# Sparse attention and a squared-ReLU layer on one core: longer DMA rows for v and k, larger mask, square and division operations, and a fifth block in the seven-product form

## The chip, the cores and the metric

The kernel runs on one core of a Trainium2 chip. The core has a matrix engine (PE, with its weight loads shown apart as PEld), a vector engine (DVE), a scalar engine (ACT), a general engine (POOL) and a queue engine (SP) that here only issues DMAs. Each takes its own instructions in order and waits for the others through semaphores. The metric is the device time of one launch in microseconds (us).

## The reference

Two stages follow each other. The first is attention over q, k and v of shape (8 batches, 8 heads, 576 positions, 64 features). Heads 0 to 3 see a band of the last 32 positions ("loc" in the code); heads 4 to 7 see every 32nd position back from the query ("str").

```
scores = q @ k^T / 8 ;  scores = where(mask, scores, -1e9)
attn   = exp(scores - max) ; attn = attn / (sum(attn) + 1e-9)
x      = (attn @ v), heads side by side : (4608 tokens, 512)
```

The second is a layer over all 4608 tokens: `h = x @ w_in` (512 to 2048), `g = s * relu(h)^2 + b`, `out = g @ w_out` (2048 to 512, fp32).

## The kernel before

All arithmetic on PE is in fp16 with fp32 sums. The tokens of the layer are cut into nine blocks T of 512 tokens. The first product of a block (F1, `ff1`, matmul at line 877) takes 16 feature tiles by four 128-row pieces of x, 64 matmuls of 512 columns. After each feature tile a ReLU out of PSUM is written to `u` (`rl`, line 899, ACT) and the square of `u` to `gT` (`sq`, line 908 on DVE, line 906 on ACT, which may take it from block `SEVEN` on). `u` has four buffers. The second product (F2, `ff2`, line 926) is again 64 matmuls of 512 columns, with an eviction on DVE (line 937) and a store for each of four token tiles. Blocks 5 to 8 (`SEVEN = 5`) do the second product in Strassen's manner (`ff2_seven`, line 845): seven products of half size, each 2 x 8 matmuls of 256 columns, out of sums of quarters of `gT` (`sums_post`, line 717, eight DVE operations a block) and differences of quarters of `w_out` (`mix_post`, line 739, four DVE operations, once, after the last plain block). Evictions of such a block are lines 764, 776 and 787.

The attention of a batch b is four pairs of heads m (0 and 1 loc, 2 and 3 str). A pair brings q and k into the layout "feature by position" (PE transposes at lines 403 and 411, or DMA transposes on SP), makes scores on PE (line 531, three groups of a PSUM bank each), takes their exponential on ACT (`ex`, line 547) and, from batch 1 on, multiplies with a 0/1 mask on DVE (`ms`, line 555), each group by itself, into one of six buffers per kind (`p_bufs`). The product with v (`av`, line 585) has a column of ones beside v, so that it also yields the sum; a reciprocal (line 600) and a multiplication (line 611) on DVE follow for each PSUM bank, one bank for a head of a loc pair, two for a head of a str pair. From batch 4 on these banks are `ps_a` and `ps_t` in turn. The result goes as x, transposed, into one of `NX = 4` slots of `xT`; the slot of batch b is free when F1 has read what lay there (`x_free`).

Loads are DMAs on POOL's queue that convert fp32 to fp16. Band k of batches 0 to 3 and all strided v of batches 0 to 3 come in long rows (several positions in one row) into a staging tile; k is then put side by side by copies (`pair_post`), v is copied into `v_str` (`cast_v`, line 315). From batch 4 on (`KB_DMA`, `LONG_V`) band k (line 270) and strided v (`load_vs`, line 298) come in rows of one position straight into their last layout, four DMAs for each tensor and batch; band k goes from there by a DMA transpose into `kT_loc`.

The order of all instructions is written by a planner (`Plan`) when the program is built. It keeps a time for each engine with assumed costs, emits PE steps one after another (attention when it is due by the progress of the layer, else F1, else F2) and gives DVE and ACT work to the engine that would end it first, in the order in which it becomes ready. On the chip every engine then keeps that order. A step of PE that comes before its inputs holds all PE work behind it.

Of the kernel before, what the change touches and what calls it, by code (L numbers as in the profile page):

```python
# [15 lines left out]
class Plan:  # L16
# [24 lines left out]
    def flush(self):  # L41
        while True:
# [13 lines left out]
            for k in p[3]:  # L56
                if isinstance(k, Group):
                    k = ("rel", k.tag, k.n)
                soon = isinstance(k, tuple) and k[0] == "soon"
                self.done[k] = end + (6000.0 if soon else p[4] or  # L60
                                           (5500.0 if eng == "D" and end < 110000.0 else self.LAT[eng]))

    def step_ready(self, s):
        r = self.ready_at(s.needs)
        if r is None:
            return None
        if s.group is not None:
            n = self.count.get(s.group.tag, 0)
            if n >= s.group.bufs:
                k = ("rel", s.group.tag, n - s.group.bufs)  # L70
                if k not in self.done:
                    return None
                r = max(r, self.done[k])
        return r

    def emit(self, s):
        if s.group is not None:
            s.group.n = self.count.get(s.group.tag, 0)
            self.count[s.group.tag] = s.group.n + 1
# [26 lines left out]
class Step:  # L106
    def __init__(self, fn, ns, needs=(), group=None, keys=(), posts=(), after=None):
        self.fn, self.ns, self.needs, self.group = fn, ns, needs, group
        self.keys, self.posts, self.after = keys, posts, after


@with_exitstack
def kernel(
# [46 lines left out]
    up = ctx.enter_context(tc.tile_pool(name="up", bufs=4))  # L160
# [24 lines left out]
    v_str = [const.tile([SQ, 4, ST, D + 1], FP16, name=f"v_str{i}") for i in range(NV)]  # L185
# [4 lines left out]
    NX = 4  # L190
# [5 lines left out]
    def x_free(b):  # L196
# [3 lines left out]
    p_bufs = {True: [const.tile([128, 3 * LQ + WIDE], FP16, name=f"p_loc{i}") for i in range(6)],  # L200
              False: [const.tile([SQ, 5 * SQ + WIDE], FP16, name=f"p_str{i}") for i in range(6)]}
# [3 lines left out]
    ks = [const.tile([SR, 4 * ST * D], FP16, name=f"ks{i}") for i in range(2)]  # L205
# [44 lines left out]
    for i in range(NV):  # L250
        nc.vector.memset(v_loc[i][:, :, :, D:D + 1], 1.0)
        nc.vector.memset(v_loc[i][0:LPAD, :, 0, :], 0.0)
        nc.vector.memset(v_str[i][:, :, :, D:D + 1], 1.0)
    for tl in p_bufs[True]:
        nc.vector.memset(tl[:, 4 * LQ:], 0.0)
    for tl in p_bufs[False]:
        nc.vector.memset(tl[:, 4 * SQ:], 0.0)
# [4 lines left out]
    def load_qk(b):  # L262
        for name, src in (("q", q), ("k", k)):
            tl = inp.tile([LQ, NL], FP16, tag=name + "l", name=name + "l")
            loaded[b, name + "l"] = tl
            if b >= (QB_DMA if name == "q" else KB_DMA):
# [28 lines left out]
    def load_vs(b):  # L295
        vs = v_str[b % NV]
        for h in range(4):
            nc.gpsimd.dma_start(  # L298
                out=vs[:, h, :, 0:D],
                in_=v[b, 4 + h].rearrange("(p j) d -> p j d", j=ST))  # L300

# [15 lines left out]
    def pair_post(b, name, mm, key):  # L317
# [4 lines left out]
        def g(eng):  # L322
            if paired[b, name] is None:
                paired[b, name] = inp.tile([128, 2, LT, 2 * D], FP16, tag="pp", bufs=3,
# [4 lines left out]
        plan.post([key], {"A": 810, "V": 350, **({"P": 900.0} if b in (1, 2, 3) else {})}, g,  # L329
                  [("in", name + "l", b, mm)])  # L330

    def cast_v(b, loc, mm, key):
        nt, np_, dst = (LT, 128, v_loc) if loc else (ST, SQ, v_str)

        def g(eng):
            src = vl_stage if loc else loaded[b, "vs"].rearrange(
                "p (h t d) -> p h t d", h=4, d=D)
            for h in range(2 * mm, 2 * mm + 2):
                copy_on(eng, out=dst[b % NV][0:np_, h, :, 0:D], in_=src[:, h])
        n = nt * D  # L340
        plan.post([key], {"P": 1000.0} if loc else {"A": 2 * (170 + 0.83 * n), "V": 540.0}, g,
# [4 lines left out]
    def rows_before(b, mm, key):  # L346
# [5 lines left out]
        def g(eng):  # L352
# [3 lines left out]

    TB, SB, AB, F1B, F2B = 1, 2, 1, 2, 2
# [3 lines left out]
          for tag, n in (("t", TB), ("s", SB), ("a", AB), ("f1", F1B), ("f2", F2B))}  # L361

    taken = {"a": 0, "t": 0, "s": 0}

    def group_of(kind, b, m, q=False):
# [3 lines left out]
        if b == 0:  # L369
            banks = {"a": [f2, f2, f1], "t": [t, a], "s": [("s", SB), ("s", SB), f1]}[kind]  # L370
# [12 lines left out]
    def pair_steps(b, m):  # L383
# [70 lines left out]
        def k_dma(eng):  # L454
            if loc:
                st["k"] = kT_loc[mm]
                if b > KB_DMA and (b - KB_DMA) % 2:

                    if b == KB_DMA + 1:
                        loaded["kT", mm] = qkp.tile([128, ST * SR], FP16, tag="kTs", name="kT_alt")  # L460
                        nc.gpsimd.memset(loaded["kT", mm][:, 0:LPAD], 0.0)
                    st["k"] = loaded["kT", mm]
                nc.sync.dma_start_transpose(
                    out=st["k"][:, LPAD:LPAD + S].rearrange("d (t p) -> d t p", t=nt),
                    in_=loaded[b, "kl"][:, 768 * mm:768 * mm + 768])
# [3 lines left out]
            else:  # L469
                if (b, "kT2") not in loaded:  # L470
                    loaded[b, "kT2"] = inp.tile([128, 2, ST, SR], FP16, tag="vs", name="kT2")
# [4 lines left out]
        def q_dma(eng):  # L476
            if loc:
                if (b, "qTl") not in loaded:
                    loaded[b, "qTl"] = inp.tile([128, 2, LT, LQ], FP16, tag="pp", bufs=3,
# [5 lines left out]
            if (b, "qT2") not in loaded:  # L485
                loaded[b, "qT2"] = inp.tile([128, 2, ST, SR], FP16, name="qT2",
                                            **({"tag": "vs"} if b < KB_DMA else
                                               {"tag": "pp", "bufs": 3}))
# [10 lines left out]
        if k_by_dma:  # L499
# [18 lines left out]
        def score(i, group):  # L518
# [18 lines left out]
            if i % per_s == n - 1:  # L537
                key = ("s", id_, g)
                s.keys = [key]

                def ex(eng):
                    whole = p_bufs[loc][p_taken[loc] % len(p_bufs[loc])]
                    p_taken[loc] += 1
                    st["pw", g] = whole
                    pt = whole[:, 0:2 * per_s * nq].rearrange("k (t c) -> k t c", c=nq)
                    st["pt", g] = pt
                    nc.scalar.activation(  # L547
                        out=pt[0:nk, 0:2 * n].rearrange("k t c -> k (t c)"),
                        in_=st["s", g][0:nk, 0:2 * n * nq], func=AF.Exp, scale=scale)

                def ms(eng):
                    pt = st["pt", g]
                    mask = (mask_loc if loc else mask_str)[:, None, :].to_broadcast(
                        [nk, 2 * n, nq])
                    nc.vector.tensor_tensor(  # L555
                        out=pt[0:nk, 0:2 * n], in0=pt[0:nk, 0:2 * n], in1=mask, op=ALU.mult)
# [696 lines left out]
```

The softmax here doesn't subtract the row's maximum and nothing guards it: scores larger than these inputs give would overflow.

## Time and profile before

| | |
|---|---|
| median of 3 runs | 312.08 us (311.35 to 312.26) |
| profiled execution | 310.75 us, its span 309.0 us |
| PE busy | 300.5 us, 97% of the span |
| DVE, ACT, POOL busy | 218.2, 178.3, 99.8 us |
| granted TensorE clock | full in every slice |
| DMA moved | 37.28 MB in 99940 packets, 81170 of them under 512 B |

Spans are of one profiled execution. Matmuls are pipelined and their shown durations overlap, so the time that PE gives a matmul is read from the distance of starts, not from the duration. The same holds in a lesser way on DVE and ACT, where an instruction's row begins before that of its forerunner ends.

### The profile page before, as it was taken

The page shows a single profiled execution, that of the slowest core. Times are in us where ns is not written, and L with a number is a line of the kernel's source. Part 1 is how long each engine was busy: PE and PEld are TensorE (multiplying, and loading weights), DVE is VectorE, ACT ScalarE, POOL GpSimd, SP SyncE. Part 2 cuts the span into 40 slices and gives each one's busy share as a digit, 9 for nine tenths or more (in the row PEclk, how much of TensorE's full clock was granted, in tenths as well). Part 3 has the DMA queues.
Part 4 walks back from the last instruction along what each step waited for, and adds up shares of the span by engine and source line. Part 5 has one row for each costly group of instructions (what it writes and reads, how often), then busy time and mean ns, then how long its engine had stood idle before and what let it go on. Part 6 is the DMA issues. An engine that isn't in the chain of part 4 may idle for free.

```text
span 309.0 us, 6715 instructions
## 1 busy us (share of the span) xinstructions
PE 300.5 (97%) x2526; PEld 194.4 (63%) x2526; DVE 218.2 (71%) x575; ACT 178.3 (58%) x336; POOL 99.8 (32%) x146
## 2 busy tenths in 40 slices
PE   8899999989999999999999999999999999999994
PEld 3765655555656655556687755565677666766883
DVE  7567958799976877859755874589866366737653
ACT  1876945769736964668055736694945445356300
POOL 8562559934951592059202950000000000000000
PEclk9999999999999999999999999999999999999999
DMA  7999999998999699679998999842010100200313
GB/s 127 204 212 205 216 175 159 219 135 122 99 165 176 86 147 155 110 110 183 150 174 153 128 146 159 172 92 88 2 36 34 68 2 34 104 1 0 105 67 106
DMA packets 99940, 37.28 MB, mean 121 GB/s; under 512 B 81170, under 2 KB 95890, under 8 KB 99906
## 3 DMA queue, kind: packets, MB, share of 16 engines
q0 software_dynamic: 57200, 18.08, 60.9%
q1 hardware_dynamic: 42706, 18.76, 29.9%
q8 instruction: 20, 0.33, 0.5%
q14 instruction: 14, 0.11, 0.1%
HBM read 36.84 MB, written 10.32 MB: 153 GB/s over the span
## 4 chain that ended last, share of the span: by engine, by line
PE 82%; DMA 9%; DVE 4%; issue 2%; ACT 1%; POOL 1%; SPq 0%; DVEq 0%; POOLq 0%; ACTq 0%
PE ps_f L877 35%; PE ps_f L926 20%; PE ps_f L845 12%; DMA ql<-in_q_dram 6%; PE ps_s L531 4%; PE ps_a L585 2%; DMA w_out_sb<-in_v_dram 2%; PE ps_s L845 2%; PE ps_t L585 1%; PE ps_t L845 1%; PE ps_s L926 1%; PE ps_t L411 1%; DMA out_dram<-o 1%; PE ps_t L633 1%; DVE gT L908 1%
## 5 line engine op out<-in xcount | busy, mean ns | idle before, releaser
L877 PE MATMUL ps_f<-xT,w_in_sb 128*128 128x512 f16 (+1 forms) x632 | 148.0, 357 | 0.0
L899 ACT ACTIVATE u<-ps_f 128x512 f16<-128x512 f32 x137 | 81.1, 596 | 72.8 <-PE ps_f L877 69.5
L877 PEld LDWEIGHTS <-w_in_sb 128*128 128x128 f16 x640 | 68.1, 113 | 34.5
L926 PE MATMUL ps_f<-w_out_sb,gT 128*128 128x512 f16 x304 | 80.7, 379 | 0.2 <-DVE gT L908 0.2
L908 DVE TENSOR_TENSOR gT<-u 128x512 f16<-128x512 f16 x111 | 48.1, 438 | 31.7 <-ACT u L899 30.6
L926 PEld LDWEIGHTS <-gT 128*128 128x128 f16 x320 | 28.9, 98 | 23.2 <-DVE gT L908 0.5
L845 PEld LDWEIGHTS <-gT 128*128 128x128 f16 x320 | 31.0, 98 | 8.7
L845 PE MATMUL ps_f<-w_out_sb,gT 128*128 128x256 f16 x184 | 25.9, 273 | 0.0
L611 DVE TENSOR_TENSOR x_nat<-ps_a,rec 72x256 f16<-72x256 f32 (+1 forms) x52 | 23.7, 456 | 0.6
L547 ACT ACTIVATE p_loc<-ps_s 128x384 f16<-128x384 f32 x46 | 21.1, 493 | 5.1 <-PE ps_s L531 4.8
L547 ACT ACTIVATE p_str<-ps_s 72x432 f16<-72x432 f32 (+1 forms) x46 | 21.0, 485 | 3.2 <-PE ps_s L531 2.9
L585 PEld LDWEIGHTS <-p_str 72*128 72x128 f16 x256 | 15.5, 98 | 11.2 <-issue 1.4
L906 ACT ACTIVATE gT<-u 128x512 f16<-128x512 f16 x33 | 20.8, 630 | 1.0
L293 POOL DMA_DIRECT2D v_loc<-in_v_dram x28 | 20.6, 764 | 1.8 <-DVE qD_loc L315 1.8
L937 DVE SCALAR_TENSOR_TENSOR o<-ps_f,s_sb,bcs 128x512 f32<-128x512 f32 x19 | 14.1, 747 | 9.4 <-PE ps_f L926 9.2
L298 POOL DMA_DIRECT2D v_str<-in_v_dram x16 | 13.0, 815 | 10.7 <-PE ps_a L585 3.7
L555 DVE TENSOR_TENSOR p_str<-p_str,mask_str 72x432 f16<-72x432 f16 (+1 forms) x42 | 14.7, 360 | 1.3 <-ACT p_str L547 1.0
L555 DVE TENSOR_TENSOR p_loc<-p_loc,mask_loc 128x384 f16<-128x384 f16 x42 | 14.6, 360 | 1.2 <-ACT p_loc L547 0.9
L845 PEld LDWEIGHTS <-S 128*128 128x128 f16 x128 | 12.5, 98 | 3.2
L315 ACT COPY xT<-ps_t 128x576 f16<-128x576 f16 x9 | 5.7, 637 | 13.4 <-PE ps_t L633 13.4
L600 DVE RECIPROCAL rec<-ps_a 72x4 f32<-72x4 f32 (+1 forms) x52 | 9.1, 176 | 6.1 <-PE ps_a L585 5.5
L585 PEld LDWEIGHTS <-p_loc 128*128 128x128 f16 x192 | 10.1, 98 | 5.2 <-issue 0.7
(158 smaller groups left out, 406.4 us busy)
## 6 DMA issues: line engine op xcount, KB each, us to landing
out_dram<-o SPq DMA_DIRECT2D x34, 256.0 KB, 3.1
w_out_sb<-in_moe_w_out_dram POOLq DMA_DIRECT2D x4, 512.0 KB, 11.1
v_loc<-in_v_dram POOLq DMA_DIRECT2D x28, 72.0 KB, 7.8
ql<-in_q_dram POOLq DMA_DIRECT2D x6, 288.0 KB, 6.4
qs<-in_q_dram POOLq DMA_DIRECT2D x6, 288.0 KB, 6.2
ks<-in_k_dram POOLq DMA_DIRECT2D x6, 288.0 KB, 7.6
kl<-in_k_dram POOLq DMA_DIRECT2D x4, 288.0 KB, 8.9
kl<-in_k_dram POOLq DMA_DIRECT2D x16, 72.0 KB, 3.9
```

The lines of the kernel that those rows point to most:

```text
L293: nc.gpsimd.dma_start(out=vl[LPAD:128, h, :, 0:D], in_=v_band(b, h))
L547: nc.scalar.activation(out=pt[0:nk, 0:2 * n].rearrange("k t c -> k (t c)"), in_=st["s", g][0:nk, 0:2 * n * nq], func=AF.Exp, scale=scale)
L555: nc.vector.tensor_tensor(out=pt[0:nk, 0:2 * n], in0=pt[0:nk, 0:2 * n], in1=mask, op=ALU.mult)
L585: nc.tensor.matmul(out=st["a"][:, j % per, :], lhsT=st["pw", g][0:nk, i * nq:i * nq + WIDE], rhs=vt[0:nk, 2 * mm + e, j, :])
L611: nc.vector.tensor_tensor(out=st["x"][:, j0:j0 + per, 64 * e:64 * e + 64], in0=st["pa", e, j][0:nq, 0:per, 0:D], in1=st["rec", e, j][0:nq, ...
L845: nc.tensor.matmul(out=gts[name, T, t][:, 0] if halves else gts[name, T][:, t], lhsT=lhs(k, t), rhs=rhs(k), start=fresh and k == 0 and (ha ...
L877: nc.tensor.matmul(out=gts["h", T, ft][:, lo:hi], lhsT=w_in_sb[min(ft // 4, 2)][:, ct].rearrange("p (c x l) -> p c l x", x=128, l=4)[:, ma ...
L899: nc.scalar.activation(out=gts["u", T, ft], in_=gts["h", T, ft], func=AF.Relu)
L906: nc.scalar.activation(out=gts[T][:, ft, :], in_=u, func=AF.Square)
L908: nc.vector.tensor_tensor(out=gts[T][:, ft, :], in0=u, in1=u, op=ALU.mult)
L926: nc.tensor.matmul(out=gts[id_], lhsT=gts[T][:, ft, ts * 128:(ts + 1) * 128], rhs=w_out_sb[:, ft, cols], start=(ft == 0), stop=(ft == NFT ...
L937: nc.vector.scalar_tensor_tensor(out=o[:, 0:n], in0=gts[id_], scalar=s_sb[:, 0:1], in1=bcs[:, cols], op0=ALU.mult, op1=ALU.add)
```

## The change

- Strided v of all batches is loaded in long rows into one staging tile `vs` and copied into `v_str`, which is now one buffer instead of two; a copy waits until the product with v of the batch before has been made. `load_vs` is gone.
- Band k of all batches is loaded in long rows; from batch 4 on it is put side by side (`pair_post`, also on POOL), transposed by DMA into `kTl`, and a new copy `k_spread` on DVE or ACT brings it into `kT_loc`. The buffer `kT_alt` is gone.
- The exponentials of a pair go into one wide buffer (two per kind instead of six small ones), and one mask operation covers the pair.
- From batch 4 on a product with v fills `ps_a` and `ps_t` together, and one reciprocal and one multiplication cover both banks.
- Two feature tiles share a buffer `u` (three of double size), one square covers both, and ACT may take it in every block (`SQ_ACT = 0`).
- `SEVEN` is 4 instead of 5. `NX` is 3 instead of 4, so the wrap of the ring of x slots cuts matmuls of F1 in blocks 3 (192 and 320 columns) and 6 (384 and 128) instead of block 4 (256 and 256).
- The planner's numbers follow: squares 700 (DVE) or 1055 (ACT) for two, strided v copies 890 instead of 540, 12000 for the landing of a DMA transpose where 5500 was assumed before 110 us.

```diff
@@ Plan.flush
-                self.done[k] = end + (6000.0 if soon else p[4] or
-                                           (5500.0 if eng == "D" and end < 110000.0 else self.LAT[eng]))
+                self.done[k] = end + (6000.0 if soon else p[4] or self.LAT[eng])
@@
-    up = ctx.enter_context(tc.tile_pool(name="up", bufs=4))
+    up = ctx.enter_context(tc.tile_pool(name="up", bufs=3))
-    v_str = [const.tile([SQ, 4, ST, D + 1], FP16, name=f"v_str{i}") for i in range(NV)]
+    v_str = const.tile([SQ, 4, ST, D + 1], FP16)
-    NX = 4
+    NX = 3
-    p_bufs = {True: [const.tile([128, 3 * LQ + WIDE], FP16, name=f"p_loc{i}") for i in range(6)],
-              False: [const.tile([SQ, 5 * SQ + WIDE], FP16, name=f"p_str{i}") for i in range(6)]}
+    p_bufs = {True: [const.tile([128, 11 * LQ + WIDE], FP16, name=f"p_loc{i}") for i in range(2)],
+              False: [const.tile([SQ, 15 * SQ + WIDE], FP16, name=f"p_str{i}") for i in range(2)]}
@@ load_qk
-            if b >= (QB_DMA if name == "q" else KB_DMA):
+            if name == "q" and b >= QB_DMA:
@@
-    def load_vs(b):
-        vs = v_str[b % NV]
-        for h in range(4):
-            nc.gpsimd.dma_start(
-                out=vs[:, h, :, 0:D],
-                in_=v[b, 4 + h].rearrange("(p j) d -> p j d", j=ST))
@@ pair_post
-                paired[b, name] = inp.tile([128, 2, LT, 2 * D], FP16, tag="pp", bufs=3,
+                paired[b, name] = inp.tile([128, 2, LT, 2 * D], FP16, tag="pp", bufs=5,
@@ cast_v
-        plan.post([key], {"P": 1000.0} if loc else {"A": 2 * (170 + 0.83 * n), "V": 540.0}, g,
+        free = [("a", (b - 1, 2 + mm), 1, ST - 1)] if b and not loc else []
+        plan.post([key] + free, {"P": 1000.0} if loc else {"A": 2 * (170 + 0.83 * n), "V": 890.0}, g,
@@ pair_steps
+        def k_spread(eng):
+            st["k"] = kT_loc[mm]
+            copy_on(eng, out=st["k"][:, LPAD:LPAD + S].rearrange("d (p j) -> d p j", j=nt),
+                    in_=loaded[b, "kTl"][:, mm].rearrange("d j p -> d p j"))
+        if k_by_dma and loc:
+            plan.post([("in", "kl", b, mm)], {"D": 1300.0}, k_dma, [("kTl", id_)])
+            plan.post([("kTl", id_), ("s", (b - 1, m), 2)], {"V": 757.0, "A": 660.0}, k_spread,
+                      [("k", id_)])
@@ score
                 def ms(eng):
-                    pt = st["pt", g]
+                    pt = st["whole"][:, 0:2 * nt * nq].rearrange("k (t c) -> k t c", c=nq)
                     mask = (mask_loc if loc else mask_str)[:, None, :].to_broadcast(
-                        [nk, 2 * n, nq])
+                        [nk, 2 * nt, nq])
+                free = [("a", (b - 1, m), 1, nt - 1)] if b else []
+                if b >= PE_MASK and g == ng - 1:
+                    s.posts.append(([("e", id_, x) for x in range(ng)],
+                                    {"V": 150 + 0.52 * 2 * nt * nq}, ms,
+                                    [("p", id_, x) for x in range(ng)]))
@@ av
+        def both_banks(e, group):
+            got = ps_at[0:nq, :, 0:per * (D + 1)].rearrange("q u (j d) -> q u j d", d=D + 1)
+            def rc(eng):
+                ...
+                nc.vector.reciprocal(out=st["rec", e][0:nq, :, 0:per], in_=got[:, :, :, D:D + 1])
+            def mu(eng):
+                ...
+                nc.vector.tensor_tensor(
+                    out=x, in0=got[:, :, :, 0:D],
+                    in1=st["rec", e][0:nq, :, 0:per].to_broadcast([nq, 2, per, D]), op=ALU.mult)
@@
+    SQ_ACT = 0
-    SEVEN = 5
+    SEVEN = 4
@@ ff1
             def sq(eng):
-                u = gts["u", T, ft]
+                u = gts["u", T, pair]
+                g = gts[T][:, pair[0]:pair[0] + 2, :]
...
-            s.posts = [([key] + free, {"A": 600, **({"V": 690} if T == 0 else {})}, rl, [("u", T, ft), group]),
-                       ([("u", T, ft)], {"V": 430, **({"A": 600} if T >= SEVEN else {})}, sq, [("g", T, ft)])]
+            s.posts = [([key] + free, {"A": 600, **({"V": 690} if T == 0 else {})}, rl, [("u", T, ft), group])]
+            if at % 2:
+                s.posts.append(([("u", T, x) for x in pair],
+                                {"V": 700, **({"A": 1055} if T >= SQ_ACT else {})}, sq,
+                                [("g", T, x) for x in pair]))
@@ fetch_v
-        if b < LONG_V:
-            early_v(b)
-        else:
-            load_vs(b)
-            arrive(both("vs", b), landing(5000))
+        early_v(b)
```

## The prediction

> **What bounds the kernel now.** I read the page first: busy shares, slices, chain.
>
> ```profile
> span 309.0 us, 6715 instructions
> PE 300.5 (97%) x2526; PEld 194.4 (63%) x2526; DVE 218.2 (71%) x575; ACT 178.3 (58%) x336; POOL 99.8 (32%) x146
> ...
> PE   8899999989999999999999999999999999999994
> ...
> DVE  7567958799976877859755874589866366737653
> ...
> PE 82%; DMA 9%; DVE 4%; issue 2%; ACT 1%; POOL 1%; SPq 0%; DVEq 0%; POOLq 0%; ACTq 0%
> ```
>
> PE is full from slice 4 on, and the chain runs through PE for 82%. A busy PE may still wait, so I next took windows and the starts of PE's rows. In a window the columns are length, then busy time (instructions) of PE, weight loads, DVE, ACT, POOL, then clock, DMA share, GB/s.
>
> ```profile
> 60.00:90.00 30.00, 28.57 (x254) 17.09 (x254) 27.62 (x73) 22.12 (x46) 19.57 (x27) 1.00 1.07 132
> 90.00:120.00 30.00, 30.00 (x254) 17.49 (x253) 22.51 (x73) 18.48 (x36) 14.25 (x23) 1.00 1.52 140
> ...
> 150.00:181.00 31.00, 31.00 (x265) 23.50 (x263) 21.05 (x60) 14.95 (x29) 12.97 (x20) 1.00 1.43 152
> 181.00:213.00 32.00, 32.00 (x230) 17.70 (x228) 22.42 (x66) 21.51 (x40) 1.32 (x2) 1.00 1.16 136
> ```
>
> Only 60 to 90 us has a PE with gaps, and there DVE is busy 27.62 of 30. The timeline shows two of the gaps and a forerunner:
>
> ```profile
> 60.57 1.73 DVE L315 COPY v_str<-vs 72x512 f16<-72x512 f16 x4
> ...
> 62.81 0.35 PE L585 MATMUL ps_a<-v_loc,p_loc 128*128 128x65 f16 x6 [0.20 <-DVE x_nat L611]
> ...
> 65.88 0.42 PE L411 MATMUL ps_t<-ident,ks 72*128 72x72 f16 x8 [0.66 <-DVE qD_str L315]
> ```
>
> Taken from start to start, PE loses beyond its usual pace 0.32 us at 46.6, 0.25 at 59.7, 0.36 at 62.2, 0.82 at 64.8, 0.48 at 75.9 and 0.33 at 84.8, together 2.6 us; from 85 us to its end it loses next to nothing. So after 85 us time can only be won by giving PE less to do.
>
> **What a matmul costs PE.** The chain in order of time (start, length, rows) gives the pace:
>
> ```profile
> 118.11 2.16 PE ps_f L926 x10
> ...
> 236.53 4.04 PE ps_f L845 x37
> ```
>
> A matmul of 512 columns takes 0.216 us, one of 256 columns 0.109.
>
> **Part 1, block 4 by seven products.** 64 x 0.216 = 13.8 us become 7 x 16 = 112 x 0.109 = 12.2 us: **-1.6 us** on PE, on the path. It also needs sums of quarters of `gT` and has more evictions; they are in part 3.
>
> **Part 2, three slots of x.** F1 of block 4 was cut into 128 halves and kept pace:
>
> ```profile
> 155.34 1.91 PE L877 MATMUL ps_f<-xT,w_in_sb 128*128 128x256 f16 x16
> 157.09 0.38 PE L926 MATMUL ps_f<-w_out_sb,gT 128*128 128x512 f16 x1
> ...
> 205.72 0.35 PE L585 MATMUL ps_t<-v_loc,p_loc 128*128 128x65 f16 x6
> 205.91 0.38 PE L926 MATMUL ps_f<-w_out_sb,gT 128*128 128x512 f16 x1
> ```
>
> 16 starts in 1.75 us, 0.109 each; 128 of them are 0.1 us more than 64 whole ones. Now two blocks are cut, the smallest piece 128 columns. Six matmuls of 65 columns, each with its own 128-column weights, start within 0.19 us, 0.032 each, so weights do not hold a piece of 128 columns: **+0.1 us**. [...]
>
> The second question is whether x comes late when F1(b-2) must have freed its slot. Stores of the loc x of batches 5, 6, 7 are issued on SP at 142.5 and 145.3, 174.9 and 182.5, 205.5 and 208.0; F1 of blocks 3, 4, 5, which now free those slots, ends at 144.8, 176.4, 208.2. A store is put back by 2.7 us at most, lands 9.3 us after issue (median), and F1 of blocks 5, 6, 7 begins at 181.2, 213.4, 240.3. Hidden: 0. What is queued behind the store on SP are stores of `out` and transposes for the next batch, none awaited within 20 us.
>
> **Part 3, DVE and ACT.** Larger operations save only what an operation costs besides its elements, and in a full queue that is less than the rows suggest, since an instruction's row begins before the last one ends:
>
> ```profile
> 34.22 0.63 DVE L555 TENSOR_TENSOR p_loc<-p_loc,mask_loc 128x384 f16<-128x384 f16 x2
> ...
> 40.02 0.42 DVE L908 TENSOR_TENSOR gT<-u 128x512 f16<-128x512 f16 x1
> 40.36 0.37 DVE L555 TENSOR_TENSOR p_str<-p_str,mask_str 72x432 f16<-72x432 f16 x1
> ...
> 53.43 0.72 DVE L611 TENSOR_TENSOR x_nat<-ps_f,rec 72x256 f16<-72x256 f32 x2
> ...
> 221.01 1.29 DVE L717 TENSOR_TENSOR gT<-gT 128x1024 f16<-128x1024 f16 x2
> ```
>
> A square takes its place for 40.36 - 40.02 = 0.34 us (its row says 0.44); 1024 elements take 1.29 - 0.685 (mean row) = 0.605. A pair saves 0.075, 72 pairs 5.4 us. Per element that is 0.52 ns, so a mask of 1152 takes 0.28 + 768 x 0.00052 = 0.68 for three of 0.28: 0.16 each, 28 times, 4.5 us. Divisions from batch 4 on: 24 reciprocals fewer at 0.1, and 24 multiplications merged at 0.05, 3.6 us. Sum 13.5 us less. [...]
>
> Added for batches 4 to 7: 16 v copies at 0.2 to 0.4 (start distance, mean row), 8 pair copies at 0.34 on DVE (0.93 on POOL), 8 `k_spread` copies for which no row has the form, bounded by 0.30 (`qD_loc` from `qTl`, 64x576) and 0.74 (`kT_loc` from PSUM, 128x576); I take 0.6, as the strided write is that of the latter. That is 8 to 15 us. The seven-product form of block 4 adds eight sums at 0.605, three evictions (seven for four) at 0.67 and one addition at 0.6, 7.5 us. So DVE and ACT get 2 to 9 us more over the launch. POOL issues 24 DMAs fewer (0.75 to 0.82 each, 19 us), and in place of 18432 rows of one position DMA carries 2688 long ones; nothing on PE waited for either after 85 us, so 0.
>
> None of this is on the path after 85 us as long as DVE and ACT have room: 21 to 22.5 of 30 us on DVE, 15 to 21.5 on ACT. Before that (batches 1 and 2, no new copies) about eight masks and ten squares save 8 x 0.16 + 10 x 0.075 = 2.0 us of DVE, against 27.6 busy. The planner also reckons the four v copies at 60.57 nearer to what they took (890 for two; 1.73 us for four rows, where it had 1080). But an AV now waits for the mask of a whole pair, and a block's first squares for two ReLUs, up to 0.7 us later each; `ps_a` and `ps_t` are no longer used in turn, so a division has to end before the next product with v. I take 0.9 of the 2.6 us as won, and 0.3 as lost to new short waits; the ends are 2.6 won and, if all waits stay and as many come, 2.6 lost.
>
> **Part 4, the new waits.** A v copy waits for the product with v of the batch before; products with v of successive batches are some 30 us apart (one batch per block from 90 us on), so it has that long. The DMA into the one staging tile waits on POOL for those copies; behind it stand the loads of the batch after next. The 12000 in place of 5500 delays only what the planner thinks of x of batches 2 and 3; F1 of block 2 begins at 94.7, and loc x of batch 2 was issued at 66.9 and 76.6, 18 us before. 0.
>
> **Sum.** -1.6 + 0.1 - 0.9 + 0.3 = -2.1 us. The profiled execution took 310.75 (span 309.0 and 1.75 around it), 1.33 below the median; 310.75 - 2.1 = 308.65, and on the median's scale 312.08 - 2.1 = **310.0 us**.
>
> **Rivals.**
> - *The early gaps close altogether* (13%): all 2.6 us won, nothing lost: -1.6 + 0.1 - 2.6 = -4.1, **308.0**. For it: DVE is what 60 to 90 us waits for and loses 2 us of work. Against: fewer, longer operations make single waits longer.
> - *Nothing left* (14%): the seven-product gain is eaten by new waits of 0.7 to 2.4 us, **311.2 to 313.0**; the measurement tells 0.3% (0.94 us) from no change. For it: every order is written anew, and the present one has no loss after 85 us, so any mistake costs.
> - *Slower: DVE becomes the bound while block 4 is done* (18%). Unlike blocks 5 to 8, block 4 falls together with attention: scores run until 210 us, products with v until 223. Into 181 to 213 us, with 22.4 busy on DVE, come eight sums (4.8), three evictions and the addition (2.6), the four differences of `w_out` and that of the bias (5.2, now after block 3), copies of one batch (about 2.7), less 2.2 saved: 35.5 us of work for 30.4. ACT has 9 us free there and may take squares (0.63 each for 512). If it takes none, PE waits 5.1 us: 312.1 - 1.6 + 5.1 = **315.6**. It decides from 2.5 us of waiting on. Against: four of the eight pair squares on ACT bring DVE to 33.1, and the back-to-back starts are 0.08 below the rows for some 70 operations, 5.6 us of room.
> - The change doing nothing at all is no case: 112 matmuls of 256 columns replace 64 of 512 by construction.
>
> **Numbers.** 55% for the forecast, whose own range is 309 to 311. Faster by over 0.3%: 55 + 13 = 68%; same 14%; slower 18%. The range takes in the closed gaps and their spread below, and half of the slower case: 307.6 to 314.0.
>
> **What would show it.** Right: 448 + 112 = 560 weight loads on the seven-product line and 256 on the plain one; their pace 0.109; PE gaps between 46 and 90 us of about 1.5 us; no gap in F1 of blocks 3 and 6. Masks near 0.75 us a row, 28 of them. Wrong: PE waiting on `gT`, on `w_mix` or on `x_nat` between 175 and 215 us; F1 of block 5, 6 or 7 waiting for x; a pace of cut matmuls above their columns; first F1 later than 18.6 us, or the start of F1 of block 1 (58.7, which waits for x of batch 1) later by more than the 2 us of F2 that then still stood.

## The result and the profile after

| | before | after |
|---|---|---|
| median | 311.72 us (311.12 to 312.26, 4 runs) | 333.52 us (331.69 to 335.39, 4 runs) |
| ratio | | 1.07 (95% interval 1.0636 to 1.0765) |
| profiled execution | 310.75 us, span 309.0 | 331.69 us, span 329.8 |

The change makes the kernel 21.8 us slower; forecast were 310.0 us and 307.6 to 314.0. The page of the kernel after:

```profile
span 329.8 us, 6676 instructions
PE 305.3 (93%) x2641; PEld 204.2 (62%) x2641; DVE 213.8 (65%) x434; ACT 192.9 (58%) x332; POOL 82.3 (25%) x121
...
PE   7789899797788899999999999799999999999995
...
PEclk9699999999999999999999999999999999999999
...
PE 82%; DVE 8%; ACT 6%; DMA 2%; issue 2%; DVEq 0%; POOLq 0%
```

No engine became the bound: DVE has 4.4 us less work than before and POOL 17.5 less, and ACT, with 14.6 more, is busy for 58% of the span. But PE, which had been full from slice 4 on, has slices of 7 and 8 among its first 14 (up to 115 us) and one of 7 at 206 to 214 us, and in one slice the granted clock falls to 0.6. DVE and ACT now hold 14% of the chain, against 5% before. The windows (columns as in the prediction: busy time and instructions of PE, weight loads, DVE, ACT, POOL, then clock, DMA share, GB/s) show where it happens:

```profile
60.00:90.00 30.00, 24.68 (x220) 13.97 (x219) 19.84 (x46) 18.62 (x34) 9.52 (x15) 1.00 0.73 108
90.00:120.00 30.00, 25.19 (x208) 13.91 (x207) 19.49 (x46) 17.70 (x31) 8.73 (x13) 1.00 0.82 119
120.00:150.00 30.00, 30.00 (x280) 20.24 (x279) 21.84 (x52) 25.23 (x44) 10.07 (x16) 1.00 0.96 123
150.00:181.00 31.00, 31.00 (x252) 19.80 (x251) 20.88 (x43) 21.77 (x40) 7.52 (x11) 1.00 1.35 153
181.00:213.00 32.00, 30.41 (x215) 17.25 (x212) 25.93 (x44) 22.68 (x39) 11.68 (x17) 1.00 1.23 161
```

From 60 to 120 us PE, DVE and ACT all have room at the same time: they wait for each other. From 120 to 181 PE is full. The starts of F1 (its first weight load in each block) say the same. F1 of block 0 begins at 24.3 us (before: 18.6), of block 1 at 69.6 (58.7), of block 2 at 111.4 (94.7), of block 3 at 140.1 (121.5); the last block of the seven-product form ends at 325.9 (304.3). So 18.6 us are lost by 140 us, and 3.0 more behind it.

The waits of PE (what waited, for whom: us in total, times, longest) name the place:

```profile
PE ps_at L412 <- DVE x_nat L651: 2.1, 5, 0.6
PE ps_at L676 <- DVE x_nat L651: 1.9, 2, 1.5
PE ps_at L620 <- ACT qD_loc L312: 1.9, 2, 1.1
PE ps_at L620 <- DVE kT_loc L312: 1.6, 3, 1.0
PE ps_at L412 <- DVE qD_str L312: 1.5, 2, 1.0
PE ps_at L404 <- ACT qD_loc L312: 1.4, 1, 1.4
```

L404 and L412 are transposes of q and k, L676 transposes of x, L620 products with v, L312 the copies out of PSUM, L651 a division. Nothing that a product with v computes is read from `qD_loc`'s or `kT_loc`'s copy; the two have only the tile `ps_at` in common. For wide divisions the change puts the banks `ps_a` and `ps_t` into one tile `ps_at` of two banks, and the waits of the program are set per tile: in the trace the writer of one bank waits for the reader of the other, below for 1.37 us, and e1 has this with the tile as its only change. The prediction, and the core of the diff ahead of it, have this tile only where a division reads it. PE's timeline of the kernel after, at the first transposes:

```profile
7.21 0.57 PE L404 MATMUL ps_at<-ident,ql 96*64 96x96 f16 x18 [0.72 <-DMA ql<-in_q_dram]
9.15 0.32 PE L404 MATMUL ps_at<-ident,ql 96*64 96x96 f16 x6 [1.37 <-ACT qD_loc L312]
...
11.16 0.69 PE L404 MATMUL ps_at<-ident,kl 96*64 96x96 f16 x12 [1.04 <-DVE qD_loc L312]
...
12.58 0.69 PE L404 MATMUL ps_at<-ident,kl 96*64 96x96 f16 x12 [0.51 <-ACT kT_loc L312]
```

and the same place before:

```profile
7.14 0.45 PE L403 MATMUL ps_a<-ident,ql 96*64 96x96 f16 x12
7.42 0.42 PE L403 MATMUL ps_t<-ident,ql 96*64 96x96 f16 x12
...
8.96 0.45 PE L403 MATMUL ps_a<-ident,kl 96*64 96x96 f16 x12 [0.47 <-ACT qD_loc L315]
...
9.50 0.45 PE L403 MATMUL ps_t<-ident,kl 96*64 96x96 f16 x12
```

Before, 24 transposes of q filled one bank and then the other without a stop. After, the last six of them, into the second bank, stand 1.37 us behind the copy out of the first. From 87 us on the same chain runs through products with v and transposes by turns:

```profile
87.49 0.29 PE L620 MATMUL ps_at<-v_str,p_str 72*128 72x65 f16 x4 [0.77 <-ACT qD_loc L312]
89.17 0.41 PE L412 MATMUL ps_at<-ident,kp 96*128 96x96 f16 x6 [0.31 <-DVE x_nat L651]
90.43 0.29 PE L620 MATMUL ps_at<-v_str,p_str 72*128 72x65 f16 x4 [0.41 <-DVE kT_loc L312]
...
95.66 0.29 PE L620 MATMUL ps_at<-v_str,p_str 72*128 72x65 f16 x4 [1.01 <-DVE kT_loc L312]
```

For the account I took the distance from each PE start to the next, took off the median of its kind, and summed what is over 0.12 us, from 5 us on (PE waits, us, in the profiled executions):

| kernel (span) | into banks a, t, before 120 us | other, before 120 | into a, t, after 120 | other, after 120 | sum |
|---|---|---|---|---|---|
| before (309.0) | 3.0 | 3.2 | 0 | 0 | 6.3 |
| after (329.8) | 19.4 | 4.7 | 0.7 | 2.3 | 27.2 |
| e1, before with a joint tile (341.6) | 19.7 | 3.4 | 11.3 | 1.2 | 35.6 |
| e2, after with separate tiles (327.3) | 1.6 | 8.0 | 0.6 | 13.0 | 23.2 |
| e3, after with a division per bank (344.3) | 18.7 | 4.5 | 11.9 | 5.6 | 40.8 |
| e10, e2 with q spread off POOL (312.5) | 1.8 | 6.5 | 0 | 3.5 | 11.8 |

Between before and after 16.4 us of the waits fall on the joint banks before 120 us, 1.5 on others there, 3.1 come after it; less 1.6 us of products that is 19.4 of the 20.8 us between the spans. The longest of the waits after 120 us is for a copy that the change adds, `k_spread`; none of them is for a copy on POOL:

```profile
213.25 0.51 PE L537 MATMUL ps_s<-qD_loc,kT_loc 128*128 128x192 f16 x4 [1.32 <-ACT kT_loc L312]
```

### The profile page after: what moved, and what is told of

It reads as the page before. It is cut to its first block, busy times and chain, and to the rows that moved or that the text cites. A ratio compares the mean times of both kernels' runs of the same rounds, so it can differ in the third digit from the quotient of the medians.

```text
span 329.8 us, 6676 instructions
## 1 busy us (share of the span) xinstructions
PE 305.3 (93%) x2641; PEld 204.2 (62%) x2641; DVE 213.8 (65%) x434; ACT 192.9 (58%) x332; POOL 82.3 (25%) x121
## 4 chain that ended last, share of the span: by engine, by line
PE 82%; DVE 8%; ACT 6%; DMA 2%; issue 2%; DVEq 0%; POOLq 0%
PE ps_f L923 33%; PE ps_f L891 15%; PE ps_f L981 14%; PE ps_s L537 4%; PE ps_at L620 4%; PE ps_at L412 2%; DMA ql<-in_q_dram 2%; PE ps_at L891 2%; PE ps_s L891 2%; ACT qD_loc L312 2%; DVE x_nat L651 1%; PE ps_at L676 1%; DVE qD_str L312 1%; ACT kT_loc L312 1%; DVE qD_loc L312 1%
## 5 line engine op out<-in xcount | busy, mean ns | idle before, releaser
L923 PE MATMUL ps_f<-xT,w_in_sb 128*128 128x512 f16 (+4 forms) x696 | 148.4, 340 | 0.0
L981 PE MATMUL ps_f<-w_out_sb,gT 128*128 128x512 f16 x240 | 63.4, 379 | 1.2 <-ACT gT L958 1.1
L960 DVE TENSOR_TENSOR gT<-u 128x1024 f16<-128x1024 f16 x44 | 30.7, 698 | 27.0 <-ACT u L950 26.5
L958 ACT ACTIVATE gT<-u 128x1024 f16<-128x1024 f16 x28 | 29.6, 1057 | 0.8
L604 DVE TENSOR_TENSOR x_nat<-ps_at,rec 72x512 f16<-72x512 f32 (+1 forms) x24 | 18.6, 774 | 0.7
L620 PEld LDWEIGHTS <-p_str 72*128 72x128 f16 x256 | 13.4, 98 | 9.1 <-issue 3.3
L537 PE MATMUL ps_s<-qD_loc,kT_loc 128*128 128x192 f16 x92 | 14.9, 255 | 1.5 <-ACT kT_loc L312 1.3
L763 DVE TENSOR_TENSOR gT<-gT 128x1024 f16<-128x1024 f16 x22 | 14.5, 682 | 1.3 <-ACT gT L958 1.3
L292 POOL DMA_DIRECT2D vs<-in_v_dram x10 | 6.8, 684 | 33.5 <-DVE rec L640 21.7
L620 PE MATMUL ps_at<-v_str,p_str 72*128 72x65 f16 x208 | 12.6, 194 | 2.6 <-DVE kT_loc L312 1.4
L891 PE MATMUL ps_f<-w_mix,gT 128*128 128x256 f16 x112 | 14.5, 272 | 0.0
L651 DVE TENSOR_TENSOR x_nat<-ps_at,rec 72x256 f16<-72x256 f32 (+1 forms) x29 | 13.2, 456 | 1.6 <-PE ps_at L412 1.2
```

The source lines that it names most:

```text
L537: nc.tensor.matmul(out=st["s", g][0:nk, c:c + 2 * nq], lhsT=(st["k"][:, i * nq:i * nq + nk] if loc else st["k"][:, i, 0:SQ]), rhs=st["q"][ ...
L604: nc.vector.tensor_tensor(out=x, in0=got[:, :, :, 0:D], in1=st["rec", e][0:nq, :, 0:per].to_broadcast([nq, 2, per, D]), op=ALU.mult)
L620: nc.tensor.matmul(out=st["a"][:, j % per, :], lhsT=st["pw", g][0:nk, i * nq:i * nq + WIDE], rhs=vt[0:nk, 2 * mm + e, j, :])
L651: nc.vector.tensor_tensor(out=st["x"][:, j0:j0 + per, 64 * e:64 * e + 64], in0=st["pa", e, j][0:nq, 0:per, 0:D], in1=st["rec", e, j][0:nq, ...
L891: nc.tensor.matmul(out=gts[name, T, t][:, 0] if halves else gts[name, T][:, t], lhsT=lhs(k, t), rhs=rhs(k), start=fresh and k == 0 and (ha ...
L923: nc.tensor.matmul(out=gts["h", T, ft][:, lo:hi], lhsT=w_in_sb[min(ft // 4, 2)][:, ct].rearrange("p (c x l) -> p c l x", x=128, l=4)[:, ma ...
```

## The experiments

Theory 1 of the first expectations is the joint tile. Theory 2 is that three slots of x, the single `v_str` and the pair-long masks and squares make attention late, theory 3 that the division over both banks holds the next product with v. From e5 on there is a fourth, that the planner's new numbers draw worse orders.

**e1: the joint tile alone, in the kernel before.** Nothing reads both banks at once; in the traces the order of instructions on PE, DVE, ACT and POOL is that of before.

```diff
-          for tag, n in (("t", TB), ("s", SB), ("a", AB), ("f1", F1B), ("f2", F2B))}
+          for tag, n in (("s", SB), ("f1", F1B), ("f2", F2B))}
+    ps_at = psum.tile([128, 2, PS], FP32, name="ps_at")
+    ps["a"], ps["t"] = [ps_at[:, 0]], [ps_at[:, 1]]
```

> The kernel before, with nothing changed but that the PSUM banks ps_a and ps_t are two halves of one tile, ps_at, as in the changed kernel; the order of instructions on PE, ACT, SP and POOL is the same as before, only waits differ. Theory 1 (uses of one bank are ordered behind uses of the other because both are one tile): about 20 us slower than before, 326 to 336 us, with the loss before 120 us, where both banks take transposes in turn, and with PE rows on ps_at that wait for a copy out of the other bank. Theory 2 (three slots of x, one v_str, pair-long masks and squares make attention late): no change, 311 to 313 us. Theory 3 (the division over both banks at once holds the next product with v): no change, 311 to 313 us.

Measured: 341.81 us (340.75 to 343.5), ratio 1.0955 (1.0937 to 1.0974); 29.8 us lost with the same instructions in the same order, by waits (35.6 us in the account, 6.3 before) and by a lower clock (the mean granted clock of the profiled execution is 0.983, before 1.0). That is more than the 326 to 336 expected. The longest of PE's waits are of the kind seen after:

```profile
PE ps_at L587 <- DVE x_nat L613: 5.8, 9, 1.2
PE ps_at L413 <- DVE x_nat L613: 4.3, 6, 1.0
PE ps_at L587 <- ACT qD_loc L315: 3.2, 4, 1.3
```

**e2: the changed kernel with separate tiles** (and so with a division per bank):

```diff
-    AV_WIDE = KB_DMA
+    AV_WIDE = B
-          for tag, n in (("s", SB), ("f1", F1B), ("f2", F2B))}
-    ps_at = psum.tile([128, 2, PS], FP32, name="ps_at")
-    ps["a"], ps["t"] = [ps_at[:, 0]], [ps_at[:, 1]]
+          for tag, n in (("t", TB), ("s", SB), ("a", AB), ("f1", F1B), ("f2", F2B))}
+    ps_at = None
```

> The changed kernel with ps_a and ps_t as two tiles again, and so with a division for each bank in every batch; all else of the change stays. Theory 1: the loss goes, 309 to 313 us, first F1 at about 18.6 us again. Theory 2: 328 to 334 us. Theory 3: 309 to 313 us. It is told from theory 3 by the next run. What is left against the kernel before is the rest of the change: -1.6 us by the prediction's part 1, up to 2.6 us of early gaps either way.

Measured: 324.25 us (322.57 to 329.08), ratio 1.039 (1.0348 to 1.0432). 9.3 us come back, not all: my expectation that the joint tile was everything fell. The waits into a and t are nearly gone (1.6 us before 120 us in the account, below the 3.0 of before), others have come late in the launch. The longest, in the timeline of POOL and then of PE (its profiled execution took 329.08 us, 4.8 above its median):

```profile
171.07 0.18 POOL L1049 COPY gate<-kT 1x1 f16<-1x1 f16 x1 [22.48 <-DMA kT<-ks]
171.87 0.18 POOL L1049 COPY gate<-kT 1x1 f16<-1x1 f16 x1 [0.62 <-DMA kT<-ks]
172.35 2.90 POOL L274 DMA_DIRECT2D ql<-in_q_dram  x4 [0.31 <-issue]
...
177.36 2.92 POOL L297 DMA_DIRECT2D v_loc<-in_v_dram  x4
180.26 0.74 POOL L292 DMA_DIRECT2D vs<-in_v_dram  x1
180.99 1.40 POOL L312 COPY qD_str<-qT 64x576 f16<-64x576 f16 x2
```
```profile
182.44 0.88 PE L535 MATMUL ps_s<-qD_str,kT 128*72 128x144 f16 x6 [5.99 <-POOL qD_str L312]
```

The gate is a copy of one element, by which POOL waits for the k transposes of a batch before it loads the next one. Behind it stand twelve DMA issues, 172.35 to 181.0, and behind those the two spreading copies of q (`q_spread`, a copy per head, which brings the transposed q into the layout for the scores) that the current batch needs. PE waited 6.0 us for them. The next longest wait, 3.2 us up to 164.99, is another: F1 waits for a ReLU, which stands on ACT behind a copy into `v_loc` whose load is late:

```profile
163.73 0.73 ACT L312 COPY v_loc<-v_loc 32x640 f16<-32x640 f16 x1 [3.66 <-DMA v_loc<-in_v_dram]
```

**e3: joint tile, a division per bank.** The changed kernel with only `AV_WIDE = B`; its order on PE, DVE, ACT and POOL is that of e2.

> The changed kernel with ps_at still one tile, but a division for each bank as before; it has the same order of instructions on PE, ACT, SP and POOL as e2_after_split and differs from it in the one tile alone. Theory 1: 328 to 336 us, some 20 us above e2_after_split. Theory 2: 328 to 334 us, the same as e2_after_split. Theory 3: 309 to 313 us, the same as e2_after_split.

Measured: 346.07 us (345.55 to 346.11), ratio 1.1087 (1.1071 to 1.1103). This is above the expected 328 to 336, but theories 2 and 3 forecast no difference from e2, and so are out for the 21.8 us between the two. The tile alone costs that here (346.07 - 324.25), and the wide divisions bring 12.5 of it back (346.07 - 333.52). They do so only where they are used, from batch 4 on: the waits into a and t after 120 us are 11.9 us in e3 and 0.7 in the changed kernel (11.3 in e1). Before 120 us, where each bank is used by itself, the three have nearly the same: 18.7, 19.4 and 19.7.

**e4: block 4 by seven products alone**, in the kernel before.

```diff
-    SEVEN = 5
+    SEVEN = 4
```

> The kernel before with block 4 by seven products too, and nothing else of the change. The prediction's part 1: 1.6 us faster than before, 310.1 us, with 560 weight loads on the seven-product line and no new gap on PE. Rival (DVE becomes the bound while block 4 is done, since it still falls together with attention): the gain is lost or turned, 311 to 316 us, with PE waiting for sums, for w_mix or for x_nat between 180 and 215 us.

Measured: 310.5 us (309.78 to 311.15), ratio 0.9953 (0.9937 to 0.9969), 1.5 us won. The windows of e4 show what the added sums did to DVE while block 4 is done, where before had 22.42 us on DVE, 32.00 on PE:

```profile
181.00:213.00 32.00, 31.79 (x265) 22.79 (x264) 27.57 (x64) 23.23 (x45) 3.39 (x4) 1.00 1.24 125
```

DVE is 86% busy, PE loses 0.2 us. The rival in which DVE becomes the bound is out for this part alone; in the changed kernel, where block 4 comes some 20 us later, DVE is busy for 25.79 us of 202 to 234.

**e5 to e7: other parts alone, in the kernel before.** e5 has only the planner's landing time:

```diff
-                self.done[k] = end + (6000.0 if soon else p[4] or
-                                           (5500.0 if eng == "D" and end < 110000.0 else self.LAT[eng]))
+                self.done[k] = end + (6000.0 if soon else p[4] or self.LAT[eng])
```

> The kernel before with the planner's landing time of transposing DMAs at 12000 throughout instead of 5500 before 110 us; no instruction is added or taken away, only orders can move. Part 4 of the prediction put this at 0: by that 311.5 to 312.5. Rival: the later landing times make the planner put products of blocks 1 and 2 and attention of batches 2 and 3 in another order, and what the separate banks left of the loss up to F1 of block 3 (5.9 us) comes from here: then 315 to 318.

Measured: 312.71 us (10 runs), against 311.76 for before beside it, ratio 1.0041 (1.002 to 1.0062): a small loss, 0.95 us between the medians, near the prediction's 0 and far from the rival. e6 has the paired squares, three buffers of `u` and three slots of x:

```diff
-    up = ctx.enter_context(tc.tile_pool(name="up", bufs=4))
+    up = ctx.enter_context(tc.tile_pool(name="up", bufs=3))
-    NX = 4
+    NX = 3
-                gts["u", T, ft] = up.tile([128, PS], FP16, tag="u", name="u")
+                if at % 2 == 0:
+                    gts["u", T, pair] = up.tile([128, 2, PS], FP16, tag="u", name="u")
...
+            if at % 2:
+                s.posts.append(([("u", T, x) for x in pair],
+                                {"V": 700, **({"A": 1055} if T >= SQ_ACT else {})}, sq,
```

> The kernel before with two parts alone: squares of two blocks of 512 in one operation (on ACT too), with three instead of four buffers of u, and three slots of x (the room for the pairs comes from the fourth). By the prediction the cut matmuls cost 0.1 us and the paired squares take 5.4 us off DVE, of which at most a part of the 2.6 us of early gaps is won: 311 to 312. Rival: a first square that waits for two ReLUs holds up F2 or the buffers of u; 3 us or more lost, 315 to 318.

Measured: 313.7 us, ratio 1.0071 (1.005 to 1.0091), 1.9 us lost; between the two. The account's waits rise from 6.3 to 9.9 us, all before 90 us: 1.4 us at 29.2 (a load of q), 0.9 at 33.5 (ACT), 1.5 together from 86.9 to 88.8. After 90 us there are none, with block 3 and block 6 of F1 cut, so the cut matmuls and x cost nothing. e7 has the masks of a pair in one operation and two buffers of p:

```diff
-    p_bufs = {True: [const.tile([128, 3 * LQ + WIDE], FP16, name=f"p_loc{i}") for i in range(6)],
+    p_bufs = {True: [const.tile([128, 11 * LQ + WIDE], FP16, name=f"p_loc{i}") for i in range(2)],
...
-                        [nk, 2 * n, nq])
+                        [nk, 2 * nt, nq])
```

> The kernel before with the masks of a whole pair in one operation and two buffers of p of each kind instead of six, alone. By the prediction DVE is relieved by 4.5 us and products with v wait up to 0.7 us longer for the first group: between 311 and 313. Rival: with two buffers the exponentials have to wait for the products with v of the batch before, and the longer mask stands between scores and products with v in the early batches: 315 to 320.

Measured: 311.31 us (10 runs), ratio 0.999 (0.9975 to 1.0006): no difference clear of noise, within the 311 to 313 expected.

**e8 and e9: without the long rows.** Strided loads of v and band k as before (`load_vs`, two buffers `v_str`, `kT_alt`, no staging, no copies); e8 from e2, e9 from the changed kernel itself.

```diff
-    v_str = const.tile([SQ, 4, ST, D + 1], FP16)
+    v_str = [const.tile([SQ, 4, ST, D + 1], FP16, name=f"v_str{i}") for i in range(NV)]
-            if name == "q" and b >= QB_DMA:
+            if b >= (QB_DMA if name == "q" else KB_DMA):
...
-        early_v(b)
+        if b < LONG_V:
+            early_v(b)
+        else:
+            load_vs(b)
+            arrive(both("vs", b), landing(5000))
```

> The changed kernel with separate banks a and t and narrow divisions (324.25) and, further, with the loads of strided v and band k as they were before (strided loads straight to their places, two buffers of strided v, no staging tile, no copies). Theory: the waits at 161 and 176 us there (3.3 and 6.0 us) come from the copies that the long rows need, of k and v, and from the DMAs that stand behind them on POOL: without them 312 to 317. Rival: the residual 12 us are of the longer masks, the paired squares or the planner's landing times: 320 to 325.

Measured: 318.57 us (314.61 to 318.74), ratio 1.0202 (1.0141 to 1.0262): 5.7 us won over e2, short of what I expected. The profiled execution is that of 314.61 us, and its one long wait can't come from the copies of the long rows, which are gone. It is again a spreading copy of q on POOL, now at 116 us, behind a load into `v_str`:

```profile
116.58 0.81 POOL L301 DMA_DIRECT2D v_str<-in_v_dram  x1 [1.21 <-ACT p_str L553]
...
117.39 1.81 POOL L318 COPY qD_str<-qT 64x576 f16<-64x576 f16 x2
```
```profile
PE ps_s L535 <- POOL qD_str L318: 3.1, 1, 3.1
```

> The changed kernel as it is, joint banks and wide divisions kept, but with the loads of strided v and band k as before (strided loads straight to their places, no copies). If the cost of the long rows (5.7 us between the two kernels with separate banks) adds to that of the joint banks: 327 to 329. Rival: the joint banks already hold PE up where the copies are late, so that taking the copies away wins less than 2 us: 331.5 to 333.5.

Measured: 330.57 us (329.23 to 332.52), ratio 1.0614 (1.0568 to 1.066): 3.0 us less than the changed kernel, between theory and rival; the intervals of the two ratios overlap, so the gain is not clear of noise. Its waits into a and t before 120 us are 15.9 us, and one of 3.6 us on POOL's copy of q has come. So without the long rows the waits at the joint tile and for POOL's copies of q are still there; in each new order the copies of q stand at another place in POOL's queue.

**e10: the spreading copies of q off POOL**, in e2; nothing else is edited.

```diff
-            plan.post([("qT", id_), ("s", (b - 1, m), 2)], {"P": 2000.0, "V": 940.0, "A": 1340.0}, q_spread,
+            plan.post([("qT", id_), ("s", (b - 1, m), 2)], {"V": 940.0, "A": 1340.0}, q_spread,
```

> The changed kernel with separate banks and narrow divisions (324.25), with the spreading copies of q kept off POOL (DVE or ACT alone may take them); POOL then gets some pair copies of k in their place. Theory: the wait of 6.0 us at 176 us, where a spreading copy of q stood on POOL behind a gate copy and the loads of the batch after, goes with the half clock that follows it: 315 to 319. Rival: the pair copies of k or a copy on DVE or ACT come as late, and as much is lost in another place: 322 to 326.

Measured: 314.66 us (314.27 to 315.84), ratio 1.009 (1.006 to 1.012). 9.6 us are won over e2, a little more than expected. That is more than the one wait of 6.0 us: the mean granted clock is 1.0 in e10's profiled execution and at least 0.995 in its others, where e2's have 0.978 to 0.989, and the order on the other engines has moved too, so that the wait of 3.2 us is gone as well. No wait of PE is longer than 1.1 us:

```profile
PE ps_f L1210 <- DVE w_mix L247: 1.1, 1, 1.1
PE ps_s L535 <- ACT kT_loc L312: 1.1, 1, 1.1
PE ps_a L402 <- DMA kl<-in_k_dram: 1.0, 1, 1.0
```

With neither the joint tile and its wide divisions nor POOL's copies of q (which the kernel before has too), all other parts of the change together stand at 1.009 of before. The parts run alone multiply to 0.9953 x 1.0041 x 1.0071 x 0.999 = 1.0055; the rest, 0.0035 or 1.1 us, is for the long rows and for what the parts do together, and lies within what the intervals leave open.

**e11 and e12: what can be kept.** The kernel before with `SEVEN = 4` and the masks of e7, and the same with `SEVEN = 3`.

> The kernel before with block 4 by seven products (310.5 alone) and with the pair-long masks (311.31 against 311.76 alone). If both gains stand: 310.0 to 310.5. Rival: the longer masks stand on DVE before the sums of block 4 and cost what was won: 311.5 or more.

Measured: 309.86 us (309.58 to 310.87), ratio 0.9933 (0.9912 to 0.9954): the fastest here, 2.2 us below the kernel before. Its interval overlaps that of e4 (0.9937 to 0.9969), so it isn't shown that the masks add anything.

> The same with block 3 by seven products as well. PE has 1.6 us less to do again: 308.4 to 309.0. Rival: block 3 falls together with attention from its start (its first layer ends at 144.8 us in the kernel before), and with eight more sums (4.8 us), three evictions and an addition (2.6 us) DVE becomes the bound between 150 and 180 us, or the differences of the weights aren't done in time: 311 to 316.

Measured: 323.08 us (322.09 to 324.36), ratio 1.0356 (1.0315 to 1.0397). The loss is even larger than the rival's 311 to 316, and its cause is not DVE's sums. The waits of PE:

```profile
PE ps_s L531 <- POOL qD_str L315: 11.4, 1, 11.4
PE ps_a L588 <- DVE x_nat L614: 1.6, 1, 1.6
PE ps_f L848 <- DVE Va L767: 1.6, 1, 1.6
```

On POOL `qD_str` starts at 184.70, behind two gates (168.5 and 169.2), the loads of the next batch from 169.75 on, and a last load of `v_str`, which itself waited 1.56 us. Why POOL stands so here and not in e11 was not followed up. The windows:

```profile
165.00:176.50 11.50, 9.75 (x101) 9.15 (x100) 8.89 (x21) 8.86 (x17) 7.11 (x12) 1.00 1.49 150
176.50:190.50 14.00, 4.35 (x29) 3.52 (x29) 0.92 (x2) 1.75 (x4) 7.97 (x11) 0.52 1.73 94
```

DVE is busy for 0.92 of 14 us while PE waits.

**Not measured.** Three kernels have no measurement: the changed kernel itself with the copies of q off POOL, e12 with them off POOL, and e10 with the old landing times. So it is open whether block 3 by seven products gains another 1.5 us once those copies are out of the way, and how the last 0.9% of e10 is divided. For the changed kernel its trace speaks for little: all PE waits after 120 us are 3.1 us there, and the list of its waits has none on POOL. A wide division without a joint tile was not tried either.

## Why the prediction was wrong

- **Part 1 (-1.6 us), right.** e4 measures -1.5. In the changed kernel the plain F2 goes from 69.0 to 55.2 us of PE starts, the seven-product line from 48.7 to 60.9, together -1.6. The line has 560 weight loads, the plain one 256.
- **Part 2 (+0.1), right.** F1 takes 124.4 us of starts before and 124.5 after. No F1 of blocks 5 to 7 waits for x; e6 has no wait after 90 us.
- **Part 3, the step that failed.** The prediction put the joint banks down as "`ps_a` and `ps_t` are no longer used in turn, so a division has to end before the next product with v", with 0.3 us for all new short waits and 2.6 as the end of the range. That reads the joint tile as a matter of wide divisions, so of batches 4 to 7. It is a matter of every use of the two banks: transposes of q and k, of x and products with v of all batches. The runs put 19.4 us of PE waits there in place of 3.0, before 120 us, while the first wide division comes at 140.3. e1 shows it with nothing else changed, e3 against e2 in the changed kernel. Taken away together with its wide divisions, the tile gives back only 9.3 of the 21.8 us, because in the new order other waits come, POOL's copies of q above all; without those too (e10) 2.6 us are left. The chain needs no busy engine, which is why looking for an engine with too much work could not find it: DVE's row fell from 71% to 65%.
- **Part 3, the sizes.** A mask of 1152 was worked out as 0.68 busy and "near 0.75 us a row"; the rows are 749 and 748 ns, 28 of them. A square of 1024 was put at 0.605 back to back, from sums with rows of 685 ns; its row is 698 ns. These were near, and worth nothing: e7 gains nothing clear of noise, and where 0.9 us of early gaps were to be won, e6 loses 1.9. Whether longer operations made single waits longer, the point named against the rival of closed gaps, isn't shown: the longest of e6's new waits is for a load of q. The `k_spread` copy, taken as 0.6, is 0.65 us on DVE but 1.14 to 1.20 on ACT, and "None of this is on the path after 85 us" does not hold for it: PE waited 1.3 us for one in the changed kernel and 1.1 in e10.
- **Part 4 (0), wrong in a smaller way.** Of the wait on POOL it said "behind it stand the loads of the batch after next". The spreading copies of q stand there too. It costs nothing in the kernel before, whose order puts them ahead, 6.0 us of PE in e2's trace; the 9.6 us between e2 and e10 are more than that wait. In the trace of the changed kernel no wait of PE on POOL shows, so this is not what made it slow. "12000 for 5500" was put at 0 and is 0.95 us alone.
- **The rivals.** *DVE becomes the bound* had the sign right and the cause wrong: by e4 it does not happen at block 4. *Nothing left* described e10's kind of loss, not this size. None of the three covered waits by a shared tile.
- **What was to show it wrong.** Two of the signs came: the first F1 is at 24.3 us instead of 18.6, and F1 of block 1 at 69.6 instead of 58.7. One of the signs of being right failed: PE's gaps between 46 and 90 us are 9.6 us by the account instead of about 1.5. These signs did not name the cause; the list of PE's waits by tile did.

## What to carry to other kernels

When a change puts two buffers into one tile so that one instruction can read both, list every use of either, everywhere in the launch, and price each as a wait for the last user of the other; the waits stay where the wide instruction is never used (19.4 us before 120 us here, the first wide division at 140.3), and DVE's load, down from 71% to 65%, did not show them. For every engine that both issues loads and makes copies, look at what stands behind its waits: a copy needed at once behind the loads of a later batch cost PE 2 to 11 us in five of these kernels (2.2 in e3, 3.1 in e8, 3.6 in e9, 6.0 in e2, 11.4 in e12). And a part of a change should be run alone: here the one part that paid (1.5 us) was hidden under 23.

## What the runs showed of the hardware

Some waits of PE were paid twice in these runs, since the granted clock went to half around them. In the changed kernel it is at half from 10.79 to 17.62 us, beginning in the second of the waits of 1.37 and 1.04 us; matmuls of 192 columns start 0.16 us apart there, 0.08 in the kernel before. The windows of the changed kernel:

```profile
6.00:10.80 4.80, 2.03 (x31) 1.03 (x30) 1.59 (x8) 1.27 (x2) 2.21 (x5) 1.00 1.27 208
10.80:17.60 6.80, 5.94 (x62) 5.44 (x62) 0.45 (x2) 3.73 (x7) 4.98 (x9) 0.50 1.25 203
```

In the 4.80 us ahead of the half clock PE's rows take 2.03 us, and no single wait is longer than 1.37 us. In e2 PE waits 0.92 and 0.97 us up to 31.03 and 33.47 us, and 6.0 us up to 182.44; the windows there:

```profile
33.00:60.00 27.00, 26.53 (x242) 16.01 (x242) 17.35 (x42) 16.39 (x30) 18.72 (x22) 0.87 1.29 170
...
176.10:182.40 6.30, 0.36 (x2) 0.09 (x1) 1.32 (x3) 1.00 (x1) 6.23 (x9) 0.82 1.52 195
182.40:187.00 4.60, 4.56 (x30) 2.90 (x30) 1.32 (x4) 2.19 (x5) 0.00 (x0) 0.51 1.62 145
```

At half, a mean of 0.87 over 27 us is about 7 us, and 0.82 and 0.51 are 2.3 us in the wait and 4.5 us behind it. In e12 the mean is 0.52 from 176.50 to 190.50 us, while the copies that end the wait of 11.4 us are done at 186.10. Nor did every such wait bring it: e6 has waits of 1.2 and 0.8 us around 30 us and a mean clock of 1.0, and e8's profiled execution, with a wait of 3.1 us and a mean clock of 0.999, took 314.61 us, its other three, with 0.989 to 0.994, took 318.4 to 318.7. What decides it no run here shows.

What waits set by a tile of two banks cost by themselves, e1 shows: 29.8 us against a tile for each bank.
